# A first pair by plain products, and new places for the pieces of convolution, norm and transposes, in a convolution and SwiGLU kernel

One core of one Trainium2 chip. The metric is the time of one execution in microseconds (us) on the device; times of a kernel are medians of its runs, and a ratio is the mean time of one kernel's fast runs over that of the other's in the same rounds, so it is not quite the ratio of the two medians.

## What is computed

`x` is 8 x 4096 x 192, float32. A causal convolution with 7 taps (softmax of the weights, one set for each of 8 groups of 24 channels) is followed by a feed-forward block on the 32768 tokens:

```python
out = np.einsum('hk,bskhg->bshg', w, x_unf)          # convolution over 7 taps
rms = np.sqrt(np.mean(x * x, axis=-1, keepdims=True) + 1e-06)
xn = x / rms * rms_g
g = xn @ w_gate                                      # 192 -> 1536
silu = g * (1.0 / (1.0 + np.exp(-g)))
return (silu * (xn @ w_val)) @ w_out                 # 1536 -> 192
```

The weights come as float64 and are converted to float32 on the core.

## The kernel before

The kernel takes the tokens in 32 "pairs" of two blocks, A and B, of 512. For each pair the *front* makes the normalised activations: convolution (ACT multiplies, DVE adds), norm, transposes on DVE, a store to DRAM (`xd`) and a fetch from there (`xb`), which puts channels on partitions. Then follow four *units* (gate on the lower, value on the upper half of the array, each one a quarter of the 1536 columns) and an *output phase* (`outer`). A unit needs 18 products of a block of weights with a block of activations; here a scheme of the kind of Strassen's makes do with 16, at the price of sums of activations (`xc`, `x_sums`) and of weights (`w_sums`, once). The front of pair p+2 is cut into pieces by `yield`, and these are put between the instructions of pair p's output phase and of pair p+1's units by calls of `side(s)`.

```python
def unit(u, side):                       # 16 products; copies on ACT, results on DVE
    mm(9, d, blk(B3), True); side(1)
    mm(12, c, cs(SS), True); keep("e", c); side(2)
    mm(10, d, cs(W)); res(3, d, "e", op=ALU.add); side(3)
    ...

def outer(p, hts, side):
    for g in range(2):
        if g == 0:
            for j in range(4):
                mms(g, j, free[j], 0, range(0, FC - NF))
                ...                                          # cut: the last unit's left-over multiply
                side(j * 2); side(j * 2 + 1)                 # sides 0 to 7
            for j in range(4):
                mms(g, j, free[j], 0, range(FC - NF, FC))
                evac(o_sb[:, j, :], free[j], D)              # the first four evictions
            side(8); side(9); side(10)
        else:
            for j in range(4):
                mms(g, j, free[2 + j // 2], (j % 2) * D, range(FC))  # needs free[2], free[3]
                if j % 2:
                    evac(...)
                for s in range(3):
                    side(11 + 3 * j + s)
        ...

for p in range(PAIRS):                   # cut: the first pair also steps the conversions
    hts = []
    for u in range(NU):
        def side(s):
            if s in (3, 6, 10, 13):
                step(nxt)
        hts.append(unit(u, side))
    done(nxt)
    nxt = front(p + 2)
    sums = x_sums(p + 1)
    def aside(s):
        if s == 0:
            fetch(p + 1)
        if 9 <= s <= 12:
            step(sums)
        else:
            step(nxt, 2)
    outer(p, hts, aside)
    done(sums)
```

## Time and profile before

"Steady pair" is the mean distance from one output phase's first product to the next, pairs 2 to 30, from the starts of instructions in the trace; units and output phase are its two parts, parted at the end of the output phase's last product.

| | before |
|---|---|
| time | 3009.20 us |
| profiled span | 3003.4 us |
| PE busy | 95% of the span |
| first product, first output phase start at | 53.4, 172.1 us |
| steady pair | 90.32 us: units 58.36, output phase 31.96 |
| last pair's period, no front of a later pair beside it | 86.2 us |

PE is the array (PEld its weight loads), DVE the vector, ACT the scalar and POOL the GpSimd engine; SP's queue issues most transfers. The prediction below quotes the views and says how they are read.

### The profile page before, as it was taken

What the parts mean: (1) busy time and instruction counts of PE and PEld (TensorE: products, weight loads), DVE (VectorE), ACT (ScalarE), POOL (GpSimd) and SP (SyncE); (2) the same over time, 40 slices, a digit from 0 to 9 for tenths busy, and PEclk for the clock granted to TensorE, in tenths of its full rate; (3) what the DMA queues carried; (4) which work ended last, traced back from release to release, by engine and by line L of the source; (5) the groups of instructions that cost most, each with busy time, mean ns of one, the idle gap of its engine ahead of it and who ended that gap; (6) DMA issues with size and microseconds to landing.
All of it is one profiled execution on the core that took longest, in us unless ns stands there. A gap on an engine that the chain in (4) does not pass through costs nothing.

```text
span 3003.4 us, 53275 instructions
## 1 busy us (share of the span) xinstructions
PE 2863.6 (95%) x20480; PEld 2329.1 (78%) x20480; DVE 2164.4 (72%) x3240; ACT 2007.4 (67%) x4791; POOL 499.5 (17%) x445
## 2 busy tenths in 40 slices
PE   1699999999999999999999999999999999999999
PEld 1378778788777888878788777888877888778887
DVE  7867777677777667777667777677777677776664
ACT  5466676776676676676676767666767766766733
POOL 4821111111111111111111111111111111111110
PEclk9799999999999999999999999999999999999999
DMA  5112121222121221121221211121211121211110
GB/s 142 50 51 51 48 56 40 61 51 52 48 56 40 55 57 48 51 54 42 53 59 40 59 47 50 51 62 38 57 50 52 51 61 38 56 49 53 33 43 12
DMA packets 94895, 155.20 MB, mean 52 GB/s; under 512 B 6896, under 2 KB 64240, under 8 KB 90552
## 3 DMA queue, kind: packets, MB, share of 16 engines
q1 hardware_dynamic: 92736, 147.05, 18.9%
q0 software_dynamic: 1344, 4.72, 0.6%
q8 instruction: 160, 2.62, 0.4%
q14 instruction: 95, 0.78, 0.1%
q10 hardware_dynamic: 560, 0.03, 0.0%
HBM read 101.44 MB, written 50.33 MB: 51 GB/s over the span
## 4 chain that ended last, share of the span: by engine, by line
PE 87%; ACT 6%; DVE 5%; POOL 1%; DMA 1%; issue 1%; SPq 0%; DVEq 0%
PE ps L441 54%; PE ps L541 33%; ACT sq L330 3%; DVE y L319 2%; ACT m L315 2%; DVE sg L458 1%; ACT tp L449 1%; ACT o_sb L549 0%; POOL wf L240 0%; DMA x_sb<-in_x_dram 0%; DMA xb<-xd 0%; DVE ht L464 0%; DVE nt L364 0%; DVE ht L204 0%; DVE y L306 0%
## 5 line engine op out<-in xcount | busy, mean ns | idle before, releaser
L441 PE MATMUL ps<-xc,wf 64*128 64x512 f32 x5120 | 1612.1, 599 | 69.8 <-DVE sg L458 64.6
L441 PE MATMUL ps<-xb,wf 64*128 64x512 f32 x3072 | 1151.5, 608 | 65.7 <-POOL wf L240 56.3
L441 PEld LDWEIGHTS ps<-xc,wf 64*128 64x128 f32 x5120 | 863.5, 189 | 407.4 <-issue 157.7
L541 PE MATMUL ps<-wo_sb,ht 64*128 64x192 f32 x12288 | 1022.7, 323 | 0.0
L541 PEld LDWEIGHTS ps<-wo_sb,ht 64*128 64x128 f32 x12288 | 1016.3, 186 | 7.8 <-issue 0.3
L449 ACT COPY tp<-ps 128x512 f32<-128x512 f32 x1280 | 697.7, 584 | 182.8 <-PE ps L441 177.3
L441 PEld LDWEIGHTS ps<-xb,wf 64*128 64x128 f32 x3072 | 540.9, 191 | 254.5 <-issue 74.9
L461 ACT ACTIVATE sg<-sg 128x512 f32<-128x512 f32 x768 | 486.6, 634 | 331.0 <-DVE sg L458 330.0
L458 DVE TENSOR_TENSOR sg<-ps,tp 128x512 f32<-128x512 f32 x640 | 436.5, 682 | 287.6 <-ACT tp L449 205.2
L473 POOL TENSOR_TENSOR tp<-tp,sg 128x512 f32<-128x512 f32 x128 | 173.6, 1356 | 2401.9 <-ACT tp L449 1976.3
L315 ACT ACTIVATE m<-x_sb,taps 128x192 f32<-128x192 f32 x1520 | 539.0, 442 | 9.8 <-DMA x_sb<-in_x_dram 6.3
L319 DVE TENSOR_TENSOR y<-y,m 128x1536 f32<-128x1536 f32 x190 | 334.6, 1761 | 274.6 <-ACT m L315 274.4
L464 DVE TENSOR_TENSOR ht<-ht,sg 128x512 f32<-128x512 f32 x768 | 528.9, 715 | 0.0
L458 DVE TENSOR_TENSOR ht<-ps,tp 128x512 f32<-128x512 f32 x640 | 433.8, 678 | 2.7 <-PE ps L441 2.4
L549 ACT COPY o_sb<-ps 128x192 f32<-128x192 f32 (+1 forms) x192 | 71.3, 371 | 340.4 <-PE ps L541 340.4
L550 DVE TENSOR_TENSOR o_sb<-ps,o_sb 128x192 f32<-128x192 f32 (+1 forms) x192 | 81.5, 424 | 177.6 <-ACT o_sb L549 177.6
L473 POOL TENSOR_TENSOR tp<-tp,ht 128x512 f32<-128x512 f32 x128 | 177.8, 1389 | 0.0
L458 DVE TENSOR_TENSOR sg<-tp,ps 128x512 f32<-128x512 f32 x128 | 87.5, 684 | 66.4 <-ACT tp L449 64.2
L330 ACT ACTIVATE sq<-y 128x192 f32<-128x192 f32 x256 | 93.2, 364 | 62.6 <-DVE y L319 56.6
L348 ACT ACTIVATE y<-y,r 128x192 f32<-128x192 f32 x252 | 100.8, 452 | 39.6 <-POOL r L339 39.6
L364 DVE STREAM_TRANSPOSE nt<-y 128x256 f32<-128x256 f32 x192 | 99.6, 620 | 0.8 <-ACT y L348 0.8
L315 ACT ACTIVATE y<-x_sb,taps 128x192 f32<-128x192 f32 x248 | 88.6, 439 | 2.1 <-DVE nt L364 2.1
(50 smaller groups left out, 548.2 us busy)
## 6 DMA issues: line engine op xcount, KB each, us to landing
xb<-xd SPq DMA_DIRECT2D x128, 384.0 KB, 6.4
x_sb<-in_x_dram SPq DMA_DIRECT2D x24, 1344.0 KB, 6.5
xd<-nt SPq DMA_DIRECT2D x128, 192.0 KB, 3.2
out_dram<-o_sb SPq DMA_DIRECT2D x64, 384.0 KB, 3.2
x_sb<-in_x_dram SPq DMA_DIRECT2D x8, 1176.0 KB, 9.6
o_sb<-in_moe_w_out_dram POOLq DMA_DIRECT2D x12, 192.0 KB, 3.8
x_sb<-in_x_dram SPq DMA_DIRECT2D x8, 157.5 KB, 3.2
ht<-in_moe_w_gate_dram SPq DMA_DIRECT2D x6, 192.0 KB, 11.3
```

Of the source, the lines that this page charges most:

```text
L315: nc.scalar.mul(m[:, :, hs], xk[:, :, hs], taps[:, h, k : k + 1])
L319: nc.vector.tensor_tensor(out=y[:], in0=y[:], in1=m[:], op=ALU.add)
L330: nc.scalar.activation(out=sq[:], in_=y[:, j, :], func=AF.Square, accum_out=ss[:, j : j + 1])
L348: nc.scalar.mul(y[:, j, :], y[:, j, :], r[:, j : j + 1])
L364: nc.vector.transpose(out=nv[:, c], in_=yv[:, c])
L441: nc.tensor.matmul(out=bank(h, bk)[:], lhsT=wf[u][rows, at[i], :], rhs=rhs, start=first, stop=True, skip_group_check=True,)
L449: nc.scalar.copy(out=t[:], in_=bank(h, bk)[:])
L458: nc.vector.tensor_tensor(out=dst, in0=in0, in1=in1, op=op)
L461: nc.scalar.activation(out=og[o][:], in_=og[o][:], func=AF.Silu)
L464: nc.vector.tensor_tensor(out=ov[o], in0=ov[o], in1=og[o][:], op=ALU.mult)
L473: nc.gpsimd.tensor_tensor(out=t[:], in0=sb["a", h][:], in1=o3, op=ALU.add)
L541: nc.tensor.matmul(out=bank(h, bk)[:, w : w + D], lhsT=hts[f // NF][HALF[h], g, f % NF, j * P : (j + 1) * P], rhs=wo_sb[HALF[h], f, :], st ...
```

## The change

It means to start the array earlier and to keep it from idling where a unit begins. (1) The first pair takes the plain 18 products, which need no sums; the sums of weights are made later on POOL. (2) Half of the first norm's squares go to DVE, and a step of the weight conversion is fused. (3) More of the next front runs in the output phase, less in the units; transposes become six pieces instead of two; `x_sums` moves from sides 9 to 12 (after the first four evictions) to sides 5 and 6 (ahead of them). (4) A third product buffer, paid for with one copy buffer.

```diff
-    prods = ctx.enter_context(tc.tile_pool(name="prods", bufs=2))
-    tps = ctx.enter_context(tc.tile_pool(name="tps", bufs=12))
+    prods = ctx.enter_context(tc.tile_pool(name="prods", bufs=3))
+    tps = ctx.enter_context(tc.tile_pool(name="tps", bufs=11))
... (conversion: two instructions fused; w_sums no longer part of convert_in)
@@ norm
+        na = NJ // 2 if fast else NJ
... (ACT squares the first na of NJ; if fast, DVE multiplies and reduces the rest)
@@ place
             nc.vector.transpose(out=nv[:, c], in_=yv[:, c])
-            if c % 3 == 2:
-                yield
+            yield
+    def plain(u, side):
+        for g in (1, 0):
+            for f in range(NF):
+                bk = free[n % 4]
+                ... (3 x 2 products into the bank, silu on ACT, multiply on DVE)
+                side(n)
@@ first pair
+    for u in range(NU):
+        def side(s):
+            step(cin, 2)
+            step(cout, 3)
+            step(nxt, 2)
+            step(ws)
+        hts.append(plain(u, side))
+        done(ws)
+        ws = w_sums(u)
+        done(cin)
+        cin = convert_in(u + 2)
@@ steady pairs
+    pieces = [3] * 5 + [2] * 3 + [3] * 4 + [2] + [0] * 4 + [1] * 6
-                elif s in (3, 6, 10, 13):
+                    if s == 3 and u == 3 or s in (7, 13) and u < 3:
                         step(nxt)
@@ aside
-            if 9 <= s <= 12:
-                step(sums)
-            else:
-                step(nxt, 2)
+            if p == 0:
+                step(ws)
+            if 5 <= s <= 6:
+                step(sums, 2)
+            step(nxt, pieces[s])
```

More of the change, by code (lines that the diff above doesn't have):

```diff
@@ L203, in convert @@
         yield
-        nc.vector.tensor_scalar(
-            out=hi, in0=hi, scalar1=31, scalar2=31,
-            op0=ALU.logical_shift_right, op1=ALU.logical_shift_left,
-        )
-        yield
-        nc.vector.tensor_tensor(out=exp, in0=exp, in1=hi, op=ALU.bitwise_or)
+        nc.vector.scalar_tensor_tensor(
+            out=exp, in0=hi, scalar=0x80000000, in1=exp,
+            op0=ALU.bitwise_and, op1=ALU.bitwise_or,
+        )
         yield
@@ L274, in convert_in @@
         yield from convert(nc.vector, raw.pop(("in", u)), exp_i[:], mf_i[:], dst, rg_sb)
-        yield from w_sums(u)
     def convert_out():
@@ L328, in norm @@
         sq = work.tile([P, D], F32, name="sq")
-        for j in range(NJ):
+        na = NJ // 2 if fast else NJ
+        for j in range(na):
             nc.scalar.activation(
@@ L334, in norm @@
                 yield
+        if fast:
+            s2 = prods.tile([P, NJ, D], F32, name="m")
+            nc.vector.tensor_tensor(
+                out=s2[:, na:, :], in0=y[:, na:, :], in1=y[:, na:, :], op=ALU.mult
+            )
+            nc.vector.tensor_reduce(out=ss[:, na:], in_=s2[:, na:, :], axis=AX.X, op=ALU.add)
         r = work.tile([P, NJ], F32, name="r")
@@ L364, in place @@
             nc.vector.transpose(out=nv[:, c], in_=yv[:, c])
-            if c % 3 == 2:
-                yield
+            yield
         xd = scr[p] = dram.tile([D, PT], F32, name="xd")
@@ L533, in unit @@
         return ht
+    def plain(u, side):
+        ht = big.tile([P, 2, NF, T], F32, name="ht")
+        n = 0
+        for g in (1, 0):
+            for f in range(NF):
+                bk = free[n % 4]
+                n += 1
+                for k in range(KP):
+                    for h in range(2):
+                        nc.tensor.matmul(
+                            out=bank(h, bk)[:], lhsT=wf[u][HALF[h], k * NF + f, :],
+                            rhs=xb[HALF[h], g, k, :], start=(k == 0), stop=(k == KP - 1),
+                            skip_group_check=True,
+                        )
+                sg = sgs.tile([P, T], F32, name="sg")
+                nc.scalar.activation(out=sg[:], in_=bank(0, bk)[:], func=AF.Silu)
+                nc.vector.tensor_tensor(
+                    out=ht[:, g, f, :], in0=bank(1, bk)[:], in1=sg[:], op=ALU.mult
+                )
+                side(n)
+        return ht
     def outer(p, hts, side):
@@ L597, with side @@
     cin = convert_in(0)
+    nm = norm(0, True)
+    step(nm, 2)
     step(cin, 3)
-    done(norm(0, True))
-    step(cin)
+    done(nm)
     done(place(0))
     fetch(0)
-    nxt = front(1)
-    for _ in range(3):
-        step(nxt, 5)
-        step(cin, 2)
     done(cin)
-    done(x_sums(0))
     cin = convert_in(1)
     cout = convert_out()
-    for p in range(PAIRS):
-        hts = []
-        for u in range(NU):
-            def side(s):
-                if p == 0:
-                    step(cin)
-                    step(cout)
-                    step(nxt)
-                elif s in (3, 6, 10, 13):
-                    step(nxt)
-            hts.append(unit(u, side))
-            if p == 0:
-                done(cin)
-                cin = convert_in(u + 2)
-        if p == 0:
-            done(cout)
-        done(nxt)
+    nxt = front(1)
+    step(nxt, 5)
+    hts = []
+    ws = iter(())
+    for u in range(NU):
[9 more added lines that the diff above has]
+        cin = convert_in(u + 2)
+    done(cout)
+    done(nxt)
+    pieces = [3] * 5 + [2] * 3 + [3] * 4 + [2] + [0] * 4 + [1] * 6
+    for p in range(PAIRS):
+        if p > 0:
+            hts = []
+            for u in range(NU):
+                def side(s):
+                    if s == 3 and u == 3 or s in (7, 13) and u < 3:
+                        step(nxt)
+                hts.append(unit(u, side))
+            done(nxt)
         nxt = front(p + 2)
@@ L637, in aside @@
                 fetch(p + 1)
-            if 9 <= s <= 12:
-                step(sums)
-            else:
-                step(nxt, 2)
+            if p == 0:
[3 more added lines that the diff above has]
+            step(nxt, pieces[s])
         outer(p, hts, aside)
         done(sums)
+        done(ws)
 _INS = ['x', 'weight', 'moe_w_gate', 'moe_w_val', 'moe_w_out', 'moe_rms_g']
```

## The prediction

> **What bounds the kernel now.** I read the page first, then the busy times by stretch, the chain of waits of one pair, and the timelines of the engines around one output phase. There are 32 pairs; each is four units (16 products each, two halves of the array side by side) and an output phase ("outer").
>
> ```profile
> PE 2863.6 (95%) x20480; PEld 2329.1 (78%) x20480; DVE 2164.4 (72%) x3240; ACT 2007.4 (67%) x4791; POOL 499.5 (17%) x445
> PE   1699999999999999999999999999999999999999
> ```
>
> PE is the bound except in the first two slices (150 us). So two questions: what the start costs, and what PE loses in a steady pair. Stretches (length, busy time of PE, PEld, DVE, ACT, POOL, clock):
>
> ```profile
> 532.60:622.20 89.60, 88.05 (x645) 70.53 (x642) 65.41 (x99) 62.41 (x151) 12.83 (x10) 1.00 0.20 52
> 2881.66:2967.72 86.06, 86.06 (x642) 65.47 (x640) 51.31 (x87) 37.25 (x70) 10.00 (x8) 1.00 0.11 27
> ```
>
> The last pair, with no convolution beside it, takes 86.06 us and PE never idles: that is the floor. An ordinary pair takes 89.6, about 3.5 more. The chain of waits of one pair says where:
>
> ```profile
> 472.87 1.40 ACT m L315 x4
> 474.29 1.77 DVE y L319
> 478.52 0.46 ACT sq L330 x2
> 478.98 0.48 ACT tp L449
> 479.48 0.70 DVE sg L458
> 480.23 26.59 PE ps L441 x112
> ```
>
> The output phase ends near 472.4, but ACT still has the convolution's tail and the squares in its queue, so the first copy of the next unit comes at 478.98 and PE idles 1.55 us. The rest of the 3.5 is small waits, the largest about 0.6 us behind the two batches of three transposes. Some pairs lose more:
>
> ```profile
> 477.86:481.27 3.41, 1.86 (x7) 0.67 (x6) 1.29 (x2) 3.31 (x14) 0.00 (x0) 1.00 0.89 298
> 481.27:484.68 3.41, 3.41 (x11) 2.65 (x9) 1.29 (x2) 2.98 (x6) 3.19 (x4) 0.50 0.03 12
> ```
>
> Where the idle time falls within one stretch of 3.41 us, the next such stretch runs at clock 0.50 and 1.7 us are lost. The trace has this in 13 of the steady pairs; with it the mean pair is 90.3 us ((2881.66 - 172.56) / 30).
>
> Last, the path by which a pair's activations reach PE: transposes, store to DRAM (xd), fetch (xb), sums (xc). At the start, chain of waits (start, length):
>
> ```profile
> 35.38 2.95 DVE nt L364 x6
> 39.71 3.35 DMA xd<-nt
> 45.13 8.15 DMA xb<-xd
> ```
>
> From the last transpose (38.33) to the last byte fetched (53.28) are 15 us. Over all pairs, the completion stamps in the trace give 4.7 us (4.6 to 5.0) from the first store issue to the last landing, and for the fetch 6.3 us until the second half of the tokens is there and 9.9 (9.5 to 10.6) until all is. In a steady pair this is hidden, since the two steps lie far apart:
>
> ```profile
> 506.28 2.07 SPq L370 DMA_DIRECT2D xd<-nt  x4
> 530.44 2.60 SPq L388 DMA_DIRECT2D xb<-xd  x4
> ```
>
> **What the Trainium skill says.** "TensorE: Matmul & The Clock Gate", Part 1, says that the array's clock halves after an idle window of about 3.4 us and that the window runs free; the trace agrees on 3.41 us and on half speed, but here 1.55 us of idle time inside one window is enough. The same page, "Architectural detail", says that ACT and DVE are strict FIFO: what stands behind a waiting instruction waits too. The chain above agrees: ACT's copy stood behind the squares. "DMA: Bandwidth & Descriptors", "Where the ~2 µs actually goes", says that most of the fixed cost of a transfer is the receipt of its last byte; here the wait is longer, since 1.57 MB fetched in four pieces land about 1.8 us apart.
>
> **The change part by part.**
>
> *Start.* Before, the first unit waits for the sums of weights on POOL (PE starts at 53.4) and the four units last until 172 instead of 55 us, with conversion, weight sums and convolution in between. After, squares are split, but DVE does three conversion steps (0.76 us each) before its share, so norm ends about where it did; the transposes end near 38.5, the fetch of the second half lands near 49.9, and PE starts there. Plain units need 4 x 6 banks x 6 passes x 0.429 us = 61.8 us of PE. DVE is longer: per unit 6 evictions at 0.72, a conversion of inputs about 8.8 (from the rows of L175 to L216, one instruction fewer), two of output weights at 1.5, two adds at 1.76: about 19.7, so some 59 for three units, and 15.4 for the fourth, where PE bounds. POOL carries 35 us of output conversion, 12 us of sums per unit, then the norm's power, on which ACT waits in unit 3: a few us. With the slow clock of the first bank the output phase starts at about 132 instead of 172. Gain 40.
>
> *Unit starts.* 35 convolution pieces, the squares and the first scaling now lie inside the output phase, with a third product buffer. At its end ACT has two squares (1 us), the wait for POOL's power (2 us) and one scaling (0.8) left; the first copy lands about 4.9 us into the unit, its DVE pair at 6.2, against 6.0 us of products that PE has until it needs that bank. The 1.55 us fall to 0.3; transposes one at a time cost perhaps 0.5 together. Gain by itself: 1.55 + about 0.7 of half clock + 0.5 per pair.
>
> *The new wait.* Counting the generator's steps: front has 35 + 9 + 7 = 51; the output phase takes 41 and the units 7. Three remain for the end of unit 3: two transposes and the store to DRAM. The built instruction order shows it: on DVE the last two transposes stand after the fourth unit's multiplies, and the fetch follows the store directly. Moreover the sums moved from after the first four evictions to before them: DVE's order in the output phase is two convolution adds, eight sums, one add, then the four evictions. Let T be the first output matmul (441.2 in the pair shown). DVE, before:
>
> ```profile
> 442.92 1.88 DVE L464 TENSOR_TENSOR ht<-ht,sg 128x512 f32<-128x512 f32 x3
> 448.68 1.76 DVE L319 TENSOR_TENSOR y<-y,m 128x1536 f32<-128x1536 f32 x1 [3.88 <-ACT m L315]
> 456.20 0.36 DVE L550 TENSOR_TENSOR o_sb<-ps,o_sb 128x192 f32<-128x192 f32 x1 [0.62 <-ACT o_sb L549]
> 457.45 1.88 DVE L398 TENSOR_TENSOR xc<-xb 128x512 f32<-128x512 f32 x3
> ```
>
> After: two multiplies end at T+2.9, two transposes at T+4.0; store landed T+8.7; fetch complete T+18.6; the last six sums at 0.62 end T+22.4; the add (1.76) T+24.2; the third eviction T+25.1. PE's second half of the output phase writes the bank which that eviction frees, and PE is there at T+15.6 (96 passes at 0.1625). It waits **9.5 us in each pair**. So long a gap always halves the clock: resumptions after the gaps of the first pair stayed slow for 4.6, 6.2, 3.2, 5.3 and 5.1 us, so 2.4 us more are lost.
>
> *Sum per pair:* 86.1 + 9.5 + 2.4 + 0.8 = 98.8 us, against 90.3.
>
> *Total.* In the first output phase the transposes come earlier, the stall is about 5 us, so the units of pair 1 start at 132 + 31.2 + 4.8 + 2.4 = 170 (before 203.4). Then 29 x 98.8 = 2865; pair 30, which has no convolution beside it, 96.5; pair 31, with no fetch, 86.1; tail 4.6. Span 3222. The median time is 5.8 us above the profiled span: about 3228; I say 3225.
>
> **The rivals.** (a) *As intended:* the fetch is hidden, the unit gap and its half clock are gone. 163 (170 less the stall of the first pair) + 30 x 86.9 + 91, plus 6, gives about 2865. For it speaks that it was surely aimed at; against it, the 15 us chain which no pair does faster than 14.1, and the FIFO. (b) *The fetch comes in time, but the eight sums and the add still stand before the evictions:* DVE works from T+11.9 (second add) for 5.0 + 1.8 + 1.0 us, PE waits 4 us and loses 2.4: about 93.3 per pair, 3060. It needs the data 7 us earlier than I can derive. (c) *Only the start changes* and the steady pair stays at 90.3: about 2975. (d) The half clock is longer, up to 3.4 us lost, or the extra waits return inside units: 3260.
>
> **Range and chances.** With the mechanism right, 30 pairs times an error of about 1.3 us (0.3 in the stall, 0.7 in the clock, 0.5 elsewhere) is 40, and the start is uncertain by 8. Range 3170 to 3275. The stall follows from program order and from landings that hardly vary, so slower by over 2%: 0.93; within 2%: 0.03 (b); faster: 0.04 (a, c).
>
> **What would show it.** Right: in each output phase one PE gap of 9 to 10 us in the middle, ended by an eviction on DVE, which stood behind sums that waited for the DMA of xb; clock 0.50 for about 5 us after it; PE's share of the span falling to about 89%; no gap over 0.5 us at a unit's start; PE starting near 50 and the first output phase near 132. Wrong: sums that start before T+12 without a wait, evictions ending before T+16, or a steady pair under 92 us.

## The result

The changed kernel takes 3246.49 us (four runs, 3244.95 to 3247.60) against 3009.20: ratio 1.0789, interval 1.0770 to 1.0808. It is slower, within the predicted range, 21 us above the predicted time.

| | before | after |
|---|---|---|
| first product at | 53.4 | 48.0 us |
| first output phase at | 172.1 | 148.0 us |
| steady pair | 90.32 | 98.95 us |
| its units | 58.36 | 54.45 us |
| its output phase | 31.96 | 44.50 us |

So both aims were met: the start gained 24 us, and the units of each pair 3.9 us. Each output phase lost 12.5. The page of the changed kernel shows the loss everywhere, not in one place:

```profile
PE 2881.9 (89%) x20512; PEld 2284.9 (70%) x20512; DVE 2112.3 (65%) x3176; ACT 1966.1 (61%) x4743; POOL 479.4 (15%) x437
...
PE   3798888988889988889888899888898888998889
```

The waits of the changed kernel name the place; the columns are the total in us, the number of waits and the longest:

```profile
PE ps L567 <- DVE o_sb L576: 258.6, 31, 9.3
...
DVE xc L401 <- DMA xb<-xd: 125.1, 61, 12.1
```

There is one wait of PE for an eviction (L576) in each of 31 output phases, and two waits of DVE for the fetch. The chain of waits of one changed pair, which starts its output phase at T = 438.18, links them (start, length, what):

```profile
441.56 1.03 DVE nt L368 x2
...
443.95 3.30 DMA xd<-nt
...
449.39 9.24 DMA xb<-xd
...
458.72 2.51 DVE xc L401 x4
...
462.55 1.67 DVE y L316
...
464.40 0.62 DVE o_sb L576 x2
...
465.07 17.82 PE ps L567 x189
```

Read from above: the last two transposes, the store, the fetch, the sums, one convolution add, evictions, and only then the second half of the output phase. In the kernel before, the store lay in the third unit and the sums behind the evictions, so nothing of this was on the path. The same pair by stretches (length; busy time of PE, PEld, DVE, ACT, POOL, with the number of instructions; clock, DMA share, GB/s):

```profile
438.18:537.51 99.33, 89.11 (x643) 71.18 (x641) 65.30 (x99) 62.03 (x150) 12.61 (x10) 0.95 0.17 47
438.18:453.78 15.60, 15.60 (x194) 15.60 (x191) 8.43 (x11) 12.44 (x35) 0.00 (x0) 1.00 0.52 122
453.78:465.07 11.29, 1.07 (x6) 0.48 (x4) 7.61 (x13) 7.21 (x24) 0.00 (x0) 0.74 0.22 45
465.07:469.42 4.35, 4.35 (x28) 4.35 (x30) 4.14 (x4) 2.06 (x6) 0.00 (x0) 0.50 0.54 174
...
483.06:537.51 54.45, 54.45 (x256) 37.11 (x255) 43.32 (x71) 36.93 (x75) 12.61 (x10) 1.00 0.02 8
```

The first half of the output phase takes 15.60 us at full speed; then the array stands for 10.2 us of 11.29; then it works for 4.35 us at half the clock; and the units run without any idle time. This pair has the longest stall of all. From the starts and ends of PE's instructions and the trace's clock, the mean of pairs 2 to 30 is: 9.4 us idle (0.9 for a copy of ACT, then 8.5 for the eviction on DVE), and 2.7 us lost to the half clock (half of the array's busy time in the stretches at 0.50).

### The profile page after: what moved, and what is told of

Read it like the earlier page. It is cut to its first block, busy times and chain, and to the rows that moved or that the text cites. A ratio compares the mean times of both kernels' runs of the same rounds, so it can differ in the third digit from the quotient of the medians.

```text
span 3243.1 us, 53188 instructions
## 1 busy us (share of the span) xinstructions
PE 2881.9 (89%) x20512; PEld 2284.9 (70%) x20512; DVE 2112.3 (65%) x3176; ACT 1966.1 (61%) x4743; POOL 479.4 (15%) x437
## 4 chain that ended last, share of the span: by engine, by line
PE 70%; DMA 12%; DVE 11%; SPq 3%; issue 3%; POOL 1%; ACT 1%; DVEq 0%; ACTq 0%; POOLq 0%
PE ps L444 51%; PE ps L567 18%; DMA xb<-xd 8%; DMA xd<-nt 3%; DVE xc L401 3%; SPq L391 2%; DVE y L316 2%; DVE ht L461 1%; SPq L373 1%; DVE ht L467 1%; DVE nt L368 1%; DVE sg L461 1%; PE ps L548 1%; DVE o_sb L576 1%; DMA rg_sb<-in_moe_rms_g_dram 0%
## 5 line engine op out<-in xcount | busy, mean ns | idle before, releaser
L567 PE MATMUL ps<-wo_sb,ht 64*128 64x192 f32 x12288 | 1118.0, 339 | 284.8 <-DVE o_sb L576 258.6
L444 PE MATMUL ps<-xc,wf 64*128 64x512 f32 x4960 | 1364.7, 589 | 0.0
L567 PEld LDWEIGHTS ps<-wo_sb,ht 64*128 64x128 f32 x12288 | 1100.0, 199 | 307.0 <-DVE o_sb L576 267.7
L444 PEld LDWEIGHTS ps<-xc,wf 64*128 64x128 f32 x4960 | 775.5, 187 | 340.0 <-issue 5.9
L444 PE MATMUL ps<-xb,wf 64*128 64x512 f32 x2976 | 938.9, 589 | 0.0
L452 ACT COPY tp<-ps 128x512 f32<-128x512 f32 x1240 | 660.6, 589 | 253.2 <-PE ps L444 251.6
L444 PEld LDWEIGHTS ps<-xb,wf 64*128 64x128 f32 x2976 | 485.0, 187 | 196.4
L461 DVE TENSOR_TENSOR sg<-ps,tp 128x512 f32<-128x512 f32 x620 | 424.5, 685 | 279.5 <-ACT tp L452 277.8
L467 DVE TENSOR_TENSOR ht<-ht,sg 128x512 f32<-128x512 f32 x744 | 514.3, 719 | 0.0
L576 DVE TENSOR_TENSOR o_sb<-ps,o_sb 128x192 f32<-128x192 f32 (+1 forms) x192 | 72.6, 419 | 410.1 <-ACT o_sb L575 410.1
L401 DVE TENSOR_TENSOR xc<-xb 128x512 f32<-128x512 f32 x124 | 82.8, 689 | 125.1 <-DMA xb<-xd 125.1
L548 PE MATMUL ps<-xb,wf 64*128 64x512 f32 x288 | 76.4, 664 | 72.2 <-DMA xb<-xd 48.0
```

Of the source, the lines that this page charges most:

```text
L401: nc.vector.tensor_tensor(out=xc[:, o, :], in0=a, in1=b, op=op)
L444: nc.tensor.matmul(out=bank(h, bk)[:], lhsT=wf[u][rows, at[i], :], rhs=rhs, start=first, stop=True, skip_group_check=True,)
L452: nc.scalar.copy(out=t[:], in_=bank(h, bk)[:])
L461: nc.vector.tensor_tensor(out=dst, in0=in0, in1=in1, op=op)
L467: nc.vector.tensor_tensor(out=ov[o], in0=ov[o], in1=og[o][:], op=ALU.mult)
L548: nc.tensor.matmul(out=bank(h, bk)[:], lhsT=wf[u][HALF[h], k * NF + f, :], rhs=xb[HALF[h], g, k, :], start=(k == 0), stop=(k == KP - 1), s ...
```

## The experiments

Eleven kernels were run. The theory: the stall needs two things, data that come late (transposes and store left to the end of the fourth unit) and evictions that stand behind the waiting sums in DVE's queue; the rest is a half clock after the stall. Rivals: the late fetch costs by itself wherever the sums stand; the order of DVE's queue is enough by itself; the half clock is only a symptom.

| run | time, us | ratio to before (interval) |
|---|---|---|
| changed kernel | 3246.49 | 1.0789 (1.0770 to 1.0808) |
| e1 sums after evictions | 2931.61 | 0.9745 (0.9731 to 0.9760) |
| e2 early store | 3025.29 | 1.0055 (1.0040 to 1.0070) |
| e3 both | 2862.52 | 0.9516 (0.9502 to 0.9530) |
| e4 start only | 2983.09 | 0.9917 (0.9901 to 0.9934) |
| e5 e1, two buffers for y | 2862.30 | 0.9515 (0.9502 to 0.9528) |
| e6 e3, weight sums later | 2856.45 | 0.9495 (0.9482 to 0.9508) |
| e7 e3, norm first | 2858.61 | 0.9503 (0.9490 to 0.9516) |
| e8 useless products, 4.5 us | 3241.28 | 1.0772 (1.0757 to 1.0787) |
| e9 useless products, 9.1 us | 3181.66 | 1.0575 (1.0561 to 1.0590) |
| e10 e3, e6 and e7 together | 2853.36 | 0.9487 (0.9474 to 0.9500) |
| e11 e3, two product buffers | 2862.79 | 0.9520 (0.9507 to 0.9533) |

### The sums behind the evictions again

```diff
-            if 5 <= s <= 6:
-                step(sums, 2)
+            if 9 <= s <= 12:
+                step(sums)
```

> The changed kernel with one edit: the sums of activations go back behind the first four evictions of the output phase (sides 9 to 12); the fetch stays as late as it is. My theory says that the stall needs both, late data and evictions queued behind the waiting sums. Then the array does not stall in the middle of the output phase (10.3 us) and the clock is not halved (2.5 us): the pair falls from 98.95 to about 86.4 us and the time to about 2865 us (2855 to 2885). Rival 1 (the late fetch itself costs, the sums being late for whatever comes next): the wait moves to the start of the next unit, 2900 or more. Rival 2 (the store and fetch load slows the array): 3200 or more.

2931.61 us: the stall is gone, but a steady pair takes 88.72 us, not 86.4. The expectation missed by 67 us, and rival 1 could not be ruled out by this run: something late still cost some 2.4 us a pair. It was not at the next unit's start, for the units took 54.46; it was still in the output phase. The chain of waits of one of its pairs:

```profile
414.79 1.04 DVE nt L368 x2
...
415.85 2.87 ACT y L312 x8
418.72 4.88 ACT m L312 x15
...
428.98 0.62 DVE o_sb L576 x2
...
429.65 15.70 PE ps L567 x189
```

and among its waits

```profile
ACT y L312 <- DVE nt L368: 61.7, 29, 2.1
```

ACT begins the next convolution 2.1 us late in each pair, because its first result goes into the one buffer `y` that the last two transposes are still reading. ACT's copies for the evictions stand behind that convolution, and the array waits for them. This became a new theory, tested by e5.

### The store early, the sums left ahead of the evictions

```diff
-                    if s == 3 and u == 3 or s in (7, 13) and u < 3:
+                    if s == 3 and u == 3 or s in (3, 7, 13) and u < 3:
```

> The changed kernel with one edit: three pieces in each of the first three units instead of two, so that the last transpose and the store are issued early in the fourth unit and the fetch can start as soon as the array has let go of its source, as in the kernel before; the sums still stand ahead of the evictions. My theory: the DVE queue alone (eight sums and one add, 6.8 us, ahead of the evictions) leaves a stall of about 4 us and the clock is halved for some 5 us after it in most pairs: about 92.7 us per pair, 3055 us (3010 to 3080). Rival (the lateness of the fetch is the whole cause): no stall, 2865 us.

3025.29 us, 91.68 us per pair. DVE waits for the fetch three times in the whole run (5.5 us together), and yet PE waits 3.8 us for an eviction in each output phase (113.5 us, 30 times): the order in DVE's queue alone costs what was expected, 4 us:

```profile
PE ps L567 <- DVE o_sb L576: 113.5, 30, 4.1
...
DVE xc L401 <- DMA xb<-xd: 5.5, 3, 2.2
```

So the stall does not need both conditions, as the theory had it: the order alone makes a shorter one. The clock costs less than expected. Two pairs of this run, with and without a half clock:

```profile
330.99:422.84 91.85, 88.09 (x644) 71.46 (x642) 66.05 (x99) 61.78 (x150) 13.03 (x10) 0.98 0.18 50
422.84:513.00 90.16, 86.40 (x644) 69.46 (x642) 66.03 (x99) 61.78 (x150) 13.03 (x10) 1.00 0.19 52
```

They differ by 1.7 us. After a gap of 3.8 us one stretch of 3.41 us runs at half clock in most pairs (in two, 6.83 us), and in four none.

### Both

Both edits above together.

> Both edits together: early store and sums behind the evictions. My theory: no stall, about 86.3 us per pair, 2865 us, the same as with the sums moved alone to within 5 us. If the late fetch costs anything by itself, this run is faster than that one by it.

2862.52 us, against 2865 expected: ratio 0.9516. One pair of it, in the same columns:

```profile
408.85:495.17 86.32, 86.32 (x643) 69.47 (x641) 66.04 (x99) 61.89 (x150) 13.02 (x10) 1.00 0.20 54
```

PE does not idle in it. That is the floor to within 0.2 us, with the whole front of another pair beside it. So the rest of the change, without its two flaws, is worth 4.9%. The guess that e1 and e3 would agree to 5 us was wrong by 64 us, for the reason above.

### The start alone

The changed start, with buffers, transposes and pieces of the kernel before (diff not shown: it takes the "steady pairs", "aside", "place" and buffer lines of the diff back).

> The changed start (plain first pair, squares split, fused step of the conversion, sums of weights afterwards) with the steady schedule, buffers and transposes of the kernel before. The first output phase started at 148.0 us in the changed kernel and at 172.1 before, so the start alone should give 24 us: about 2985 us (2978 to 2992). If the start costs something later (sums of weights late for the second pair), the gain is smaller.

2983.09 us. The first output phase starts at 148.4, the steady pair takes 90.38 as before. The start is worth 25 us, 0.8%.

### A second buffer for y

```diff
+    ybuf = ctx.enter_context(tc.tile_pool(name="ybuf", bufs=2))
-        y = ys[p] = work.tile([P, NJ, D], F32, name="y")
+        y = ys[p] = ybuf.tile([P, NJ, D], F32, name="y")
... (on e1; the scratch of the conversion moves into xc to make room)
```

> The run with the sums moved behind the evictions kept 2.2 us per pair (88.55 instead of the 86.3 of both edits). Its chain of waits leads back from the evictions to ACT's convolution, and from its first instruction to the last two transposes (2.1 us of waiting in each pair): they still read the one buffer y that the convolution of the next pair writes. This run adds a second buffer for y to that kernel and changes nothing else in the steady pairs (the scratch of the weight conversion moves into the tile of sums to make room). If y is the cause: 86.4 us per pair, about 2865 us (2858 to 2872), although store and fetch stay late. If the late fetch is: 2931 us as before.

2862.30 us, 86.32 us per pair, the same as with the early store. So the 2.4 us of e1 were the buffer, and a late fetch costs nothing where its sums stand behind the evictions. Rival 1 falls, and so does rival 2 of e1's text, the load of the late store and fetch.

### The sums of weights later

```diff
-            step(ws)
+            if u == NU - 1:
+                step(ws)
-        done(ws)
-        ws = w_sums(u)
... (on e3; ws runs through all four w_sums, from the fourth unit on)
```

> The kernel with both edits (2862.5 us), with the sums of weights on POOL no longer interleaved with the conversion of the output weights in units 1 to 3 but begun in the fourth unit and carried on in the first output phase. My prediction put the first output phase at 132 us by adding up DVE's work; it came at 148 (150 in the kernel with both edits). Theory: POOL's queue held conversion steps behind sums of weights, DVE and ACT waited for those, and the evictions for DVE and ACT. Then the first output phase starts about 10 to 14 us earlier, and the time falls to about 2851 us; if POOL is not done with the sums when the second pair starts, 2 to 4 us of it are given back. Rival (DVE's own work or the slow clock sets the plain phase): under 4 us gained.

2856.45 us: 6.1 gained. The first output phase starts at 141.7 instead of e3's 150.1, 8.4 us earlier, so less than expected; the second pair gives 0.3 back. Of the 8.4, some 2 are spread between runs: the nine profiled runs with the changed start in the same order (the changed kernel, e1 to e5, e8, e9, e11) began that phase at 146.9 to 150.1, median 148.3, and e3's was the latest. Against the median the gain is 6.6, which fits the time. Nearly all of it lies in the third plain unit, 26.8 us instead of 31.7. In the changed kernel the queues are seen to hold each other up in the plain units. Two lines of POOL's timeline and one of DVE's:

```profile
104.58 2.35 POOL L238 TENSOR_TENSOR wf<-wf 128x128 f32<-128x128 f32 x5
...
107.39 1.51 POOL L184 TENSOR_SCALAR exp_o<-exp_o 128x384 uint32<-128x384 uint32 x1
...
108.94 1.36 DVE L204 SCALAR_TENSOR_TENSOR exp_o<-o_sb,exp_o 128x384 uint32<-128x384 uint32 x1 [1.33 <-POOL exp_o L184]
```

Five sums of weights stand ahead of a conversion step on POOL, and DVE waits for that step, with an eviction and the next unit's conversion behind it.

### Norm first

```diff
-    step(nm, 2)
+    step(nm, 3)
     step(cin, 3)
```

> The kernel with both edits (2862.5 us), with DVE's half of the squares of the first pair ahead of the three conversion steps instead of behind them. The prediction said that the split of the squares gives nothing because of those steps. If so, the norm now ends about 4 us earlier, the array starts near 44 instead of 48 us, and the time falls by about 4 us, to 2858.5 (2856 to 2861). If not (the array then waits for the weights): no change.

2858.61 us: 3.9 gained, as expected. The array starts at 45.2 instead of 48.2, and the first output phase at 144.7 (median of the others 148.3).

### Useless products in the stall

```diff
                     mms(g, j, free[j], 0, range(FC - NF, FC))
+                    if j == 3 and p < PAIRS - 1:
+                        warm(hts[0], free[3])    # WARM = 14 times two products, columns 320:512
                     evac(o_sb[:, j, :], free[j], D)
```

> The changed kernel, with 28 useless products of 192 columns per pair (written to unused columns of the bank that is evicted last, 0.1625 us for each of their 56 records, 9.1 us) that keep the array at work during the stall. The stall itself stays: evictions come as late as before. The half clock after it should go: 2.5 us per pair, some 75 us, to about 3171 us (3155 to 3190). If the half clock costs nothing beyond the stall: 3246. The results stay right.

3241.28 us. The run did not test what it was meant to: the records of the two halves of the array run side by side, one pair of them in 0.1625 us, so 56 records filled 4.5 us, not 9.1. A gap of about 5 us stayed, and the clock was halved after it.

> The run with the useless products covered only 4.5 us of the stall: with unchanged weights their records came 0.081 us apart, not 0.1625, and a gap of 5.1 us stayed, after which the clock was halved as before. Now twice as many: 112 records, 9.1 us, of a stall of about 10.3. The gap left is about 1 us, so the clock should stay whole: 2.5 us per pair less than the changed kernel, about 96.4 us, 3171 us (3155 to 3195). If the half clock costs nothing of its own: 3241 to 3246.

The explanation with unchanged weights in that text is wrong; the cause was my count of records. The amount (`WARM = 28`, 112 records, 9.1 us) is right. 3181.66 us, 64.8 less than the changed kernel or 2.2 us for each of 30 pairs. A pair of it:

```profile
635.10:731.16 96.06, 95.50 (x755) 78.57 (x753) 66.33 (x100) 62.03 (x150) 12.57 (x10) 1.00 0.20 48
```

The clock is whole, the output phase still takes 41.96 us (median) instead of e3's 31.9: the stall without its half clock. Three pairs of this run were halved all the same, those whose gaps were the longest (2.1 to 2.3 us). The half clock is a cost of its own. The 2.2 us understate it: by the clock of the two traces it fell from 2.7 to 0.2 us a pair, while the rest of the pair grew by 0.3, which is not traced.

### The fastest, and the third product buffer

e10 is e3 with e6 and e7, and with the last sums of weights spread into the second pair:

```diff
-            if p == 0:
+            if p == 0 and s <= 8:
                 step(ws)
+                    if p == 1 and u < 2 and s in (1, 6, 11):
+                        step(ws)
```

> Both edits, norm first, sums of weights later, and these spread into the first units of the second pair so that the power of the next norm does not wait behind them on POOL. Each gain was measured by itself: 2862.5 - 3.9 (norm first) - 6.1 (sums later) = 2852.5; with the second pair's start mended up to 2 us more: 2851 us (2847 to 2854), the fastest of all.

2853.36 us, ratio 0.9487 to the kernel before, faster than both kernels by 5.1% and 12.1% (2853.36 / 3246.49 = 0.879). The two gains add up; spreading the sums gave nothing more, since the second pair lost only 0.3 us.

e11 is e3 with `prods` at 2 buffers and `tps` at 12, as before the change.

> Both edits, with two product buffers (and twelve copy buffers) as in the kernel before, instead of three and eleven. The third buffer lets ACT run one convolution step further ahead of DVE. With the sums behind the evictions the add that frees a buffer always comes before ACT needs it (add of step 1 at 9 us after the output phase's start, ACT's step 3 at 10): no change, 2862.5 us (2860 to 2866). If the third buffer is needed: 2870 or more.

2862.79 us: no change, as expected. That part of the change is worth nothing where the sums stand behind the evictions.

## Why the prediction was right, and where it was not

*The new wait* was right as a mechanism: it is the chain shown above. e2, e3 and e5 take it apart: the order in the queue alone leaves a stall of 3.8 us, late data alone none once `y` has two buffers, and the two together some 10. Its size: the sum said T+4.0 for the last transpose, T+8.7 for the store, T+18.6 for the fetch, T+25.1 for the third eviction. The pair shown has 4.4 (441.56 + 1.03 - 438.18), 9.1, 20.5 and 26.8; its fetch was the slowest of all (11.2 us, median 10.3, before 9.9). In the mean of pairs 2 to 30 the third eviction ends at T+26.0: the transposes come 0.4 later and the fetch takes 0.4 longer than predicted. But the array also comes later to this wait, at T+17.6 and not T+15.6, since one product, on the lower half of the array, whose bank ACT reads, goes ahead alone after a wait of 0.9 us for ACT's copy. That wait the prediction did not have. So PE idles 8.5 + 0.9 = 9.4 us where the prediction had 9.5.

*The half clock*: 2.4 predicted; 2.7 by the trace's clock, 2.2 net by e9. The prediction's list of resumptions in the first pair leaves one out (at 92.64 us, still slow when that stretch ends at 102.39). Its reading that 1.55 us of idle time inside one stretch of 3.41 us halves the next one holds in the 13 pairs that it counts, but in two other steady pairs (3 and 24) the gap lay inside one stretch too and the clock stayed whole.

*What is left*: 0.8 predicted, at the starts of units and inside them. It is 98.95 - 9.36 - 2.66 - 86.13 = 0.80, where 86.13 is the last pair of e3, without a later front. But it is not in the units, which take 54.45 us as in that pair: 0.2 is also in e3's steady pairs, and the rest is about the time of that product alone (455.17 to 455.76 in the pair shown). So this term had the right size by luck. The sum: 98.8 predicted, 98.95 measured.

*The start* is the step that failed: "the output phase starts at about 132 instead of 172. Gain 40." It started at 148.0, a gain of 24. The first product was right (49.9 predicted, 48.0 measured), and so was the claim that the split of the squares gives nothing behind the conversion steps (e7). The mis-sized term is the plain units: I added up DVE's work (some 59 us for three of them), as if DVE never waited. From the starts of instructions, the first three units took 26.0, 24.5 and 31.7 us, 82 together. DVE waits for POOL and ACT, and these for DVE; e6 shows that the sums of weights on POOL make some 6.5 us of this. The rest, some 10 to 17 us (16 of the start's whole miss, or 82 - 59 = 23 of the three units, less 6.5), is open: the clock was at 0.72 to 0.87 in most of that time, and the engines' small waits for each other were not taken apart.

*The total*: 3225 against 3246.5. Of the 21 us, 16 are the start and about 4.5 the pairs (30 x 0.15).

*The rivals*: (a), the intended kernel at 2865, is e3 with 2862.5; it was the right number for another kernel. (b), the order of the queue alone, is e2: 4 us of stall as said, but 1.5 us of half clock in the mean instead of 2.4, and nearly nothing of the 0.8, so 3025 instead of 3060. (c), only the start, is e4 with 2983 against 2975; the prediction lists it under "faster", but 2975 is only 1.1% below 3009, so it belonged to "within 2%".

## What to carry to other kernels

When pieces of a pipeline are moved, count the steps to see which of them fall off the end: two transposes and one store that slipped behind the last unit cost a chain of 16 us that had been hidden. Before an instruction is moved ahead of an eviction in an engine's queue, ask when its data come: all that stands behind it inherits its wait, and here that was the array. Where several engines feed each other in order, the busiest engine's sum is a lower bound of a phase and not its length.

## What the Trainium skill lacked or had wrong

- "TensorE: Matmul & The Clock Gate", Part 1, halves the clock after an idle window of about 3.4 us. Here far less was enough: 1.55 us of idle time halved it for 3.41 us in 13 of the 29 steady pairs of the kernel before. The traces give no sharp threshold. Counting the idle time inside one stretch of 3.41 us (stretches laid from the clock records' own starts, after the first pair), the next stretch was halved in some cases from 1.45 us on (e1), left whole in others up to 1.99 (e2), and halved each time from 2.00 us on (e2, e8, e9 and the changed kernel). The page does not say either how long the half clock lasts after a gap of a given length: 3.41 us after 1.55 and mostly after 3.8, mostly 6.83 after 5.4 (e8), 10.24 (of which some 5.3 after work was taken up again) after 9.4.
- "DMA: Bandwidth & Descriptors", "Anatomy of one DMA", the fit for one transfer (2.0 us plus bytes over 436 GB/s, measured there on GpSimd's path): an estimate by it for the fetch of 1.57 MB is 5.6 us. Here, from SP's queue in four pieces, it took 9.5 to 11.2 us, the pieces landing about 1.8 us apart (393 KB each, about 215 GB/s). The page has nothing on a store that is fetched back at once: 4.7 us, then the 9.5 to 11.2.
